# A fused attention and highway kernel: DMA transposes kept for nine slots, a gate bias added on the matrix engine in five, and two points without loads

## The chip, the cores and the metric

The kernel runs on one core of a Trainium2 chip. The core has five engines with one instruction stream each: TensorE (PE in the profile, with its weight loads as PEld), VectorE (DVE), ScalarE (ACT), GpSimd (POOL) and SyncE (SP). Each works in its own program order and waits for the others on semaphores. DMAs are issued by POOL (all loads, which cast float32 to float16 on the way) and by SP (stores and DMA transposes). The metric is the device time of one execution in microseconds; the time of a kernel is the median of its runs.

## What is computed

Inputs are q, k, v of shape (4, 6336, 256) and the weights of a highway layer. Cut to what matters:

```python
qn = q / (norm(q, axis=1) + 1e-6);  kn = k / (norm(k, axis=1) + 1e-6)
a = softmax(kn.T @ qn / tau)          # one 256 x 256 matrix per batch
x = (v @ a).reshape(25344, 256)
H = relu(x @ w_h);  T = sigmoid(x @ w_t + b_t)
out = T * H + (1 - T) * x
```

## The kernel before, in words

There are two kinds of work per batch b of 4. **Phase 1** (`p1_tile`, L197 to L203) goes over 49 row tiles of 128 rows and a rest of 64: six matmuls per tile sum S = k'q and the Gram diagonals G, from which the norms come. Then a **chain** (`chain`, ten steps) turns S and G into the matrix mr, which holds a, a w_h and a w_t side by side: squared norms on DVE (L221), a power and an addition on POOL (`norms`, L237 and L238), the reciprocal on DVE (L242), a diagonal matrix on ACT (L251), a matmul that spreads it (cq, L264), the logits on DVE (L269), two exponentials on ACT (L280), the row sums' reciprocal on DVE (L291), the scaled rows on ACT (L300), a transpose on PE (L310), its copy (L319), the product with the weights (ah, L326) and two copies (L337, L339). The exponential needs another ACT table than the sigmoid, so two table loads of ACT stand around it.

**Main slots.** Each slot t (0 to 99, 25 per batch, two row tiles each) takes the transposed rows of v and runs `mains` three times (L435): four matmuls each into z (one of two PSUM banks in turn), h and x (a ring of three banks, `hx_tile`). Then `elementwise_ops`: ACT takes the sigmoid of z (tt, L486) and copies the bias over the bank again, so that the next matmuls into it add to the bias (L490, from btb, for slot t + 2); DVE forms th from h and tt (L498) and ux from tt and x (L503); POOL subtracts them into the output tile (L510). So z of slot t + 2 stands behind the ACT work of slot t, x of slot t behind th of slot t - 1, and h of slot t behind ux of slot t - 2.

**Transposes of v.** For slots below TD = 66, PE transposes the rows three slots ahead (`transpose`, L412, four matmuls between z and h of slot t, for slot t + 3, into a single PSUM bank vtps), and ACT (even slots) or DVE (odd ones) copies the result to SBUF as vts (`vt_copy`, L427). For slots 66 to 99 SP issues DMA transposes in eight groups (`dma_transposes`, L375 and L386, tiles vtd and vtr), which use buffers of the rings of q and k.

**Order.** The program is written out by hand, one slot after another; each engine keeps that order. Phase 1 of batch b + 1 is spread over the slots of batch b, its last tile standing in slots 18, 43 and 63. A planner at build time holds loads in the list `want`, sorted by the slot in which they are due. `next_loads` issues up to two after each slot (four ahead of the first chain), where buffers and eight load lanes allow it, and a model of the arrival times (`landed`) decides how many tiles of phase 1 stand in a slot. Chain steps are hung into the slots by `STEPS`; for the last batch the norms stand ahead of slot 64, the reciprocal ahead of 66, cq after the matmuls of 66, the logits ahead of 68, the exponentials after the elementwise work of 68, the scaled rows after that of 69, the transpose after 71, its copy ahead of 72, ah after 73 and the copies ahead of 74. Batch 3 is slots 75 to 99. The v of a batch comes in three loads of 16, 16 and 17 row tiles; v1 is the second load of batch 0, used by slots 8 to 15 and so by the transpose that stands in slot 5. v11 is the last load of all, v10 the one before it.

Of the kernel before, what the change touches and what calls it, by code (L numbers as in the profile page):

```python
# [9 lines left out]
AluOp = mybir.AluOpType  # L10
# [5 lines left out]
P = 128  # L16
# [3 lines left out]
def kernel(  # L20
# [30 lines left out]
    def spans(*sizes):  # L51
# [24 lines left out]
    P1_END = [19, 44, 64]  # L76


    TD = 66
    TGROUPS = [  # L80
        (2, 32, 8, 57), (2, 40, 9, 61), (3, 0, 8, 65), (3, 8, 8, 69),
        (3, 16, 8, 73), (3, 24, 8, 77), (3, 32, 8, 81), (3, 40, 9, 85),
    ]
    LULL = [0, 0, 1, 7]


# [47 lines left out]

    load_q(0)
    load_k(0)
    bt_sb = const_pool.tile([1, C], f32, tag="bt")
    nc.sync.dma_start(out=bt_sb, in_=moe_b_t.rearrange("(a m) -> a m", a=1))


    ident0 = const_pool.tile([P, P], f32, tag="ident0")
# [70 lines left out]
    def chain(b):  # L212
# [102 lines left out]

        def at_copy():
            at_sb = work_pool.tile([P, 2, C], f16, tag="at_sb", bufs=1, name=f"at_sb{b}")
            cp = nc.vector.tensor_copy if b == 0 else nc.scalar.copy
            cp(out=at_sb, in_=st["at"])  # L319
            st["at_sb"] = at_sb  # L320

# [43 lines left out]
    def dma_transposes(t):  # L365

        for n, (b, s0, ns, at) in enumerate(TGROUPS):
            if at != t:
                continue
            g = max(i for i in range(len(VG[b])) if VG[b][i][0] <= s0)  # L370
            o = s0 - VG[b][g][0]
            assert o + ns <= VG[b][g][1]
            tag = "qk"[n % 2] + "_in"
            vt = stream_pool.tile([P, QTILES, C], f16, tag=tag, bufs=QRING, name=f"vtd{n}")
            nc.sync.dma_start_transpose(  # L375
                out=vt[:, 0:ns, :].rearrange("p s (c r) -> p (s c) r", c=2),
                in_=v_t[VFIRST[b] + g][:, o : o + ns, :].rearrange("p s c -> p (s c)"),
            )
            for j in range(ns):
                vT_dma[b, s0 + j] = vt[:, j, :].rearrange("p (c r) -> p c r", c=2)  # L380
            note(ns, 0.0)
            if s0 + ns == VG[b][g][0] + VG[b][g][1]:
                used.add(("v", VFIRST[b] + g))
            if s0 + ns == NS:
                vr = const_pool.tile([P, 2, REM], f16, tag=f"vtr{b}", name=f"vtr{b}")
                nc.sync.dma_start_transpose(out=vr, in_=rem_t["v"][0:REM, b, :])  # L386
                vT_dma[b, NS] = vr

    def vT_of(t, u):
        b, i = divmod(t, NPAIR)  # L390
        return vT_t[t][:, u] if t < TD else vT_dma[b, 2 * i + u]
    on_dve = {t + LOOK for e, o in zip(P1_END, STEPS[1:]) for t in (e + o[4], e + o[4] + 1)}
    o_t = {}
    NSLOT = B * NPAIR
# [35 lines left out]
    def mains(t, dst, off, seeded):  # L430
        b, i = divmod(t, NPAIR)
        mr = mr_t[b]
        for u, r in enumerate(nrows(i)):
            for kt in range(2):
                nc.tensor.matmul(  # L435
                    dst[0:r, u, :], vT_of(t, u)[:, kt, 0:r], mr[:, kt, off : off + C],
                    start=(not seeded and kt == 0 and (u == 0 or i == NPAIR - 1)),
                    stop=(kt == 1 and (u == 1 or i == NPAIR - 1)),
                    skip_group_check=seeded,
                )  # L440
# [42 lines left out]
    def elementwise_ops(t, z, h, x, ps):  # L483
# [2 lines left out]
        nc.scalar.activation(out=tt, in_=z, func=Act.Sigmoid)  # L486
        if ps is not None:
            vt_copy(t + LOOK, ps)
        if t + 2 < NSLOT:
            nc.scalar.copy(out=z, in_=btb)  # L490
        th = work_pool.tile([P, 2, C], f32, tag="th", bufs=5, name=f"th{t}")
        ux = work_pool.tile([P, 2, C], f32, tag="ux", bufs=5, name=f"ux{t}")
# [41 lines left out]
    for m in range(1, len(VALL)):  # L534
        b, g = VALL[m]
        at = b * NPAIR + VG[b][g][0] // 2 - LOOK - 1
        for bb, s0, _, slot in TGROUPS:
            if (bb, s0) == (b, VG[b][g][0]):
                at = slot - 1
        dep = ("v", m - VRING) if m >= VRING else None  # L540
        want.append((at, len(want), load_v, m, dep, VG[b][g][1]))
    want.sort()
# [6 lines left out]
    landing = [0.0] * LANES  # L549
    landed = {}  # L550
    dma_at = [0.0]

    def note(tiles, now):
        dma_at[0] = max(dma_at[0], now) + tiles * TILE_US
# [4 lines left out]
        landed[key] = dma_at[0]  # L559

    def next_loads(k, now):
        while k and want:
            _, _, fn, arg, dep, tiles = want[0]
            if dep is not None and dep not in ready:
                return
            if landing[-LANES] > now + SLACK:
                return
            want.pop(0)
            fn(arg)
            note_load((fn, arg), tiles, now)  # L570
            k -= 1
# [10 lines left out]
    zbank = []  # L582
    btb = const_pool.tile([P, 2, C], f32, tag="btb")

    def seed_banks():


        btp = hx_tile("btp")
        nc.tensor.matmul(btp[:, 0, :], ones32[0:1, :], bt_sb, start=True, stop=True)
        for u in range(2):  # L590
            nc.scalar.copy(out=btb[:, u, :], in_=btp[:, 0, :])
        for i in range(2):
# [8 lines left out]
    for j in range(NS + 1):  # L601
        p1_tile(0, j)
        if j == QG[0][1][0]:
# [3 lines left out]
            load_rem("q", q)  # L607
            load_rem("k", k)
            seed_banks()
            preload_table(Act.Sqrt)  # L610
        if j == QG[0][2][0]:
            load_q(QFIRST[1])
# [33 lines left out]
    for t in range(NSLOT):  # L646
        b, i = divmod(t, NPAIR)
        ready = set(used)
        run(t, "pre")
        z = zbank[t % 2]  # L650
        mains(t, z, 2 * C, True)
        dma_transposes(t)
        ps = transpose(t + LOOK) if t + LOOK < TD else None
        h = hx_tile(f"h{t}")
        mains(t, h, C, False)
        x = hx_tile(f"x{t}")
# [35 lines left out]
                for at, (when, fn) in zip(STEPS[pb + 1], chain(pb + 1)):  # L692
                    hooks.setdefault((t + 1 + at, when), []).append(fn)

        next_loads(2, now)
        room = DEFER - sum(t >= at for at in DRAIN)
        out_now = 0
        while len(stores) > room and out_now < 2:
# [40 lines left out]
```

## Time and profile before

| | |
|---|---|
| median of 13 runs | 290.46 us (288.11 to 308.25) |
| the profiled execution: time, span in the profile | 288.66 us, 286.9 us |
| PE busy | 256.8 us (90% of the span) |
| POOL, DVE, ACT busy | 168.7, 162.5, 159.4 us |
| granted TensorE clock over the span, mean | 0.973 |
| POOL's DMA queue (loads) | 39.19 MB, 68.7% of 16 engines' span |
| SP's DMA queue (stores, DMA transposes) | 30.35 MB, 33.5% |
| transposes of v: by PE, by DMA | 66 slots (264 matmuls), 34 slots (8 groups and 2 rests) |

The profile is one execution on the hardware profiler. Busy time is by engine; a group of instructions is named by its line, engine and tiles ("zbank<-mr,vts" is a matmul of mr and vts into the bank of z). Times in a timeline count from the span's start. Where a row has a bracket, the engine stood idle that long before it, and the name behind the arrow is what ended the idle time.

### The profile page before, as it was taken

The numbers are of one execution on the slowest core, as the hardware profiler recorded it, in microseconds if no ns is written. First come the engines' busy times: TensorE is split into PE (matmuls) and PEld (weight loads), VectorE is DVE, ScalarE is ACT, GpSimd is POOL, SyncE is SP. The second block draws the span as 40 slices with busy tenths as digits, with TensorE's granted clock in tenths as the row PEclk, the third lists the DMA queues.
The fourth block names the chain that finished last, engine by engine and source line by source line (L and its number), as shares of the span: only waits on it lengthen the run. The fifth ranks groups of instructions, "written<-read, shape, count | busy, mean of one in ns | idle before, by whom it ended". The sixth has DMA issues, their size and how long they took to land. (4 is left out here: it accounts for less than half of the span.)

```text
span 286.9 us, 6644 instructions
## 1 busy us (share of the span) xinstructions
PE 256.8 (90%) x2708; PEld 222.6 (78%) x2708; DVE 162.5 (57%) x307; ACT 159.4 (56%) x286; POOL 168.7 (59%) x181
## 2 busy tenths in 40 slices
PE   0699886999999999999999999999999569999990
PEld 0479763999999877899999877899998346788870
DVE  1000034974455684766666774555568347899992
ACT  1040036853453688465656687445457388799970
POOL 8122230797564774566569774445454745899991
PEclk9999997999999999999999999999999897999996
DMA  6999999999999999999999999999999999999996
GB/s 98 210 211 213 207 214 212 212 215 219 211 219 210 285 229 270 268 306 268 250 265 221 277 243 266 261 310 258 233 159 267 179 245 283 279 355 238 278 378 235
DMA packets 32577, 69.97 MB, mean 244 GB/s; under 512 B 19105, under 2 KB 21154, under 8 KB 28066
## 3 DMA queue, kind: packets, MB, share of 16 engines
q0 software_dynamic: 10288, 39.19, 68.7%
q1 hardware_dynamic: 22258, 30.35, 33.5%
q8 instruction: 21, 0.34, 0.4%
q14 instruction: 10, 0.08, 0.1%
HBM read 78.38 MB, written 25.95 MB: 364 GB/s over the span
## 5 line engine op out<-in xcount | busy, mean ns | idle before, releaser
L510 POOL TENSOR_TENSOR o<-th,ux 128x512 f32<-128x512 f32 x96 | 123.7, 1294 | 72.0 <-DVE ux L503 61.1
L197 PE MATMUL S<-q,k 128*128 128x256 f16 x392 | 88.3, 279 | 11.5 <-DMA k<-in_k_dram 11.5
L498 DVE SCALAR_TENSOR_TENSOR th<-h,tt 128x512 f32<-128x512 f32 (+1 forms) x104 | 69.0, 667 | 51.0 <-PE h L435 26.3
L486 ACT ACTIVATE tt<-zbank 128x512 f32<-128x512 f32 x100 | 59.6, 596 | 68.8 <-PE zbank L435 65.3
L435 PEld LDWEIGHTS <-vts 128*128 128x128 f16 (+1 forms) x792 | 72.0, 98 | 9.9 <-issue 3.1
L200 PE MATMUL G<-k 128*128 128x128 f16 x392 | 77.2, 223 | 0.2 <-DVE junk L221 0.2
L503 DVE SCALAR_TENSOR_TENSOR ux<-tt,x 128x512 f32<-128x512 f32 (+1 forms) x104 | 67.9, 656 | 0.1
L490 ACT COPY zbank<-btb 128x512 f32<-128x512 f32 x98 | 58.4, 595 | 2.2
L203 PE MATMUL G<-q 128*128 128x128 f16 x392 | 55.0, 223 | 0.0
L197 PEld LDWEIGHTS <-k 128*128 128x128 f16 x392 | 39.1, 100 | 16.4 <-DMA k<-in_k_dram 12.3
L435 PEld LDWEIGHTS <-vtd 128*128 128x128 f16 x396 | 39.6, 101 | 11.3 <-issue 5.2
L435 PE MATMUL zbank<-mr,vts 128*128 128x256 f16 x264 | 40.3, 274 | 0.6 <-DVE mr L339 0.6
L200 PEld LDWEIGHTS <-k 128*128 128x128 f16 x392 | 39.1, 100 | 1.1 <-issue 0.3
L435 PE MATMUL h<-mr,vts 128*128 128x256 f16 x264 | 39.9, 273 | 0.0
L435 PE MATMUL x<-mr,vts 128*128 128x256 f16 x264 | 39.9, 273 | 0.0
L427 DVE CAST vts<-vtps 128x512 f16<-128x512 f32 x33 | 22.7, 688 | 21.3 <-PE vtps L412 21.3
L203 PEld LDWEIGHTS <-q 128*128 128x128 f16 x392 | 30.9, 100 | 2.6
L412 PE MATMUL vtps<-ident,v 128*128 128x128 f16 x260 | 25.2, 221 | 0.0
L435 PE MATMUL x<-mr,vtd 128*128 128x256 f16 x132 | 21.1, 284 | 3.5 <-DVE th L498 3.5
L221 DVE SCALAR_TENSOR_TENSOR junk<-G,ident 128x128 f32<-128x128 f32 x16 | 3.7, 287 | 35.8 <-PE G L203 35.8
L112 POOL DMA_DIRECT2D q<-in_q_dram x25 | 14.2, 567 | 12.1 <-DMA q<-in_q_dram 5.7
L412 PEld LDWEIGHTS <-v 128*128 128x128 f16 x260 | 19.8, 98 | 1.8 <-issue 0.4
(73 smaller groups left out, 165.3 us busy)
## 6 DMA issues: line engine op xcount, KB each, us to landing
out_dram<-o SPq DMA_DIRECT2D x23, 1024.0 KB, 9.7
v<-in_v_dram POOLq DMA_DIRECT2D x8, 1024.0 KB, 26.7
q<-in_q_dram POOLq DMA_DIRECT2D x15, 512.0 KB, 25.7
k<-in_k_dram POOLq DMA_DIRECT2D x15, 512.0 KB, 25.9
v<-in_v_dram POOLq DMA_DIRECT2D x4, 1088.0 KB, 24.1
q<-in_q_dram POOLq DMA_DIRECT2D x7, 576.0 KB, 19.5
k<-in_k_dram POOLq DMA_DIRECT2D x7, 576.0 KB, 19.7
out_dram<-o SPq DMA_DIRECT2D x4, 256.0 KB, 5.3
```

What stands on the lines that cost most here:

```text
L112: nc.gpsimd.dma_start(out=q_t[n][:, 0:ns, :], in_=rows(q[b])[:, s0 : s0 + ns, :])
L197: nc.tensor.matmul(S[:, c, :], kc, qq[0:nr, :], start=first and c == 0, stop=last and c == 1)
L200: nc.tensor.matmul(G[:, c, :], kc, kc, start=first and c == 0, stop=False)
L203: nc.tensor.matmul(G[:, 2 + c, :], qc, qc, start=False, stop=last and c == 1)
L412: nc.tensor.matmul(ps[:, u, c, 0 : nr[u]], vt[0 : nr[u], bass.ts(c, P)], ident[0 : nr[u], 0 : nr[u]], start=(u == 0 and c == 0), stop=(u = ...
L427: cp(out=sb, in_=ps)
L435: nc.tensor.matmul(dst[0:r, u, :], vT_of(t, u)[:, kt, 0:r], mr[:, kt, off : off + C], start=(not seeded and kt == 0 and (u == 0 or i == NP ...
L486: nc.scalar.activation(out=tt, in_=z, func=Act.Sigmoid)
L490: nc.scalar.copy(out=z, in_=btb)
L498: nc.vector.scalar_tensor_tensor(out=th[pr, us, :], in0=h[pr, us, :], scalar=0.0, in1=tt[pr, us, :], op0=AluOp.max, op1=AluOp.mult,)
L503: nc.vector.scalar_tensor_tensor(out=ux[pr, us, :], in0=tt[pr, us, :], scalar=1.0, in1=x[pr, us, :], op0=AluOp.subtract, op1=AluOp.mult,)
L510: last = sub.tensor_tensor(out=ot[pr, o0 + us.start : o0 + us.stop, :], in0=th[pr, us, :], in1=ux[pr, us, :], op=AluOp.subtract,)
```

## The change

- DMA transposes are kept for slots 66 to 74 alone (`BY_DMA`; two groups, now placed in slots 52 and 57 instead of 57 and 61). Slots 75 to 99 are transposed by PE in slots 72 to 96, and copied by DVE and ACT as in the slots below 66. Six groups and one rest of DMA transposes go.
- In slots 68 to 72 (`PE_BIAS`) the bias is put into the bank of z by two matmuls of 65 rows ahead of the four of z, instead of by the copy on ACT two slots earlier (in slots 66 to 70). The operands are prepared once, by a memset and some fifteen small DVE instructions (`bias_rows`) and three DMAs of the bias instead of one.
- `next_loads` isn't called after a slot in which the last tile of a phase 1 stands, nor after the slot behind it.
- Loads of v are held back by `V_HELD`: v10 until slot 67, v11 until slot 74. The test compares with the current slot, which is -1 ahead of slot 0, and with 0 for a load that isn't in the table. Loads behind a held one may pass it.
- The copy of the transposed softmax matrix goes from ACT to DVE in the last chain (L319). The load of the third part of batch 2's v is due three slots ahead of its first DMA transpose, and the planner counts a DMA transpose as 3.5 tiles instead of one.

In the built program the loads around slot 0 stand so on POOL: before, v1, q8, k8, q9 ahead of slot 0, and k9 and q10 after it; changed, q8, k8, q9, k9 ahead of slot 0, and v1 and q10 after it. Phase 1 of batch 1 stands in slots 3 to 18, two or three tiles in each, instead of slots 6 to 18 with three or four; the later phases are spread as before.

```diff
--- before.py
+++ after.py
@@ -76,11 +76,12 @@
     P1_END = [19, 44, 64]
 
 
-    TD = 66
-    TGROUPS = [
-        (2, 32, 8, 57), (2, 40, 9, 61), (3, 0, 8, 65), (3, 8, 8, 69),
-        (3, 16, 8, 73), (3, 24, 8, 77), (3, 32, 8, 81), (3, 40, 9, 85),
-    ]
+    BY_DMA = range(66, 75)
+    TGROUPS = [(2, 32, 8, 52), (2, 40, 9, 57)]
+
+    PE_BIAS = range(68, 73)
+
+    V_HELD = {10: 67, 11: 74}
     LULL = [0, 0, 1, 7]
 
 
@@ -134,8 +135,10 @@
 
     load_q(0)
     load_k(0)
-    bt_sb = const_pool.tile([1, C], f32, tag="bt")
-    nc.sync.dma_start(out=bt_sb, in_=moe_b_t.rearrange("(a m) -> a m", a=1))
+    bt_sb = const_pool.tile([65, C], f32, tag="bt")
+    nc.vector.memset(bt_sb, 0.0)
+    for r in (0, 32, 64):
+        nc.sync.dma_start(out=bt_sb[r : r + 1, :], in_=moe_b_t.rearrange("(a m) -> a m", a=1))
 
 
     ident0 = const_pool.tile([P, P], f32, tag="ident0")
@@ -315,7 +318,7 @@
 
         def at_copy():
             at_sb = work_pool.tile([P, 2, C], f16, tag="at_sb", bufs=1, name=f"at_sb{b}")
-            cp = nc.vector.tensor_copy if b == 0 else nc.scalar.copy
+            cp = nc.scalar.copy if 0 < b < B - 1 else nc.vector.tensor_copy
             cp(out=at_sb, in_=st["at"])
             st["at_sb"] = at_sb
 
@@ -378,7 +381,7 @@
             )
             for j in range(ns):
                 vT_dma[b, s0 + j] = vt[:, j, :].rearrange("p (c r) -> p c r", c=2)
-            note(ns, 0.0)
+            note(3.5 * ns, 0.0)
             if s0 + ns == VG[b][g][0] + VG[b][g][1]:
                 used.add(("v", VFIRST[b] + g))
             if s0 + ns == NS:
@@ -388,7 +391,7 @@
 
     def vT_of(t, u):
         b, i = divmod(t, NPAIR)
-        return vT_t[t][:, u] if t < TD else vT_dma[b, 2 * i + u]
+        return vT_dma[b, 2 * i + u] if t in BY_DMA else vT_t[t][:, u]
     on_dve = {t + LOOK for e, o in zip(P1_END, STEPS[1:]) for t in (e + o[4], e + o[4] + 1)}
     o_t = {}
     NSLOT = B * NPAIR
@@ -430,6 +433,12 @@
     def mains(t, dst, off, seeded):
         b, i = divmod(t, NPAIR)
         mr = mr_t[b]
+        if t in PE_BIAS and seeded:
+            for u in range(2):
+                nc.tensor.matmul(
+                    dst[:, u, :], ones_hl, bt_hl, start=(u == 0), stop=False,
+                    skip_group_check=True,
+                )
         for u, r in enumerate(nrows(i)):
             for kt in range(2):
                 nc.tensor.matmul(
@@ -486,7 +495,7 @@
         nc.scalar.activation(out=tt, in_=z, func=Act.Sigmoid)
         if ps is not None:
             vt_copy(t + LOOK, ps)
-        if t + 2 < NSLOT:
+        if t + 2 < NSLOT and t + 2 not in PE_BIAS:
             nc.scalar.copy(out=z, in_=btb)
         th = work_pool.tile([P, 2, C], f32, tag="th", bufs=5, name=f"th{t}")
         ux = work_pool.tile([P, 2, C], f32, tag="ux", bufs=5, name=f"ux{t}")
@@ -534,9 +543,8 @@
     for m in range(1, len(VALL)):
         b, g = VALL[m]
         at = b * NPAIR + VG[b][g][0] // 2 - LOOK - 1
-        for bb, s0, _, slot in TGROUPS:
-            if (bb, s0) == (b, VG[b][g][0]):
-                at = slot - 1
+        if (b, VG[b][g][0]) == TGROUPS[0][:2]:
+            at = TGROUPS[0][3] - 3
         dep = ("v", m - VRING) if m >= VRING else None
         want.append((at, len(want), load_v, m, dep, VG[b][g][1]))
     want.sort()
@@ -549,6 +557,7 @@
     landing = [0.0] * LANES
     landed = {}
     dma_at = [0.0]
+    slot = [-1]
 
     def note(tiles, now):
         dma_at[0] = max(dma_at[0], now) + tiles * TILE_US
@@ -559,13 +568,14 @@
         landed[key] = dma_at[0]
 
     def next_loads(k, now):
-        while k and want:
-            _, _, fn, arg, dep, tiles = want[0]
-            if dep is not None and dep not in ready:
+        while k and want and landing[-LANES] <= now + SLACK:
+            for i, (_, _, fn, arg, dep, tiles) in enumerate(want[:5]):
+                held = fn is load_v and V_HELD.get(arg, 0) > slot[0]
+                if not held and (dep is None or dep in ready):
+                    break
+            else:
                 return
-            if landing[-LANES] > now + SLACK:
-                return
-            want.pop(0)
+            want.pop(i)
             fn(arg)
             note_load((fn, arg), tiles, now)
             k -= 1
@@ -582,11 +592,37 @@
     zbank = []
     btb = const_pool.tile([P, 2, C], f32, tag="btb")
 
+
+
+    ones_hl = const_pool.tile([65, P], f16, tag="ones_hl")
+    bt_hl = const_pool.tile([65, C], f16, tag="bt_hl")
+    bt_r = const_pool.tile([65, C], f32, tag="bt_r")
+
+    def bias_rows():
+        nc.vector.memset(ones_hl.bitcast(u16), 0)
+        nc.vector.memset(bt_hl.bitcast(u16), 0)
+        part = work_pool.tile([65, C], f16, tag="bt_part", bufs=1)
+        rest = bt_sb
+        for r, one, scale in ((0, 1.0, 2.0**11), (32, 2.0**-11, 8.0), (64, 2.0**-14, None)):
+            nc.vector.tensor_scalar(
+                out=ones_hl[r : r + 1, :], in0=ones32[r : r + 1, :], scalar1=one,
+                scalar2=None, op0=AluOp.mult, op1=AluOp.bypass,
+            )
+            nc.vector.tensor_copy(out=part, in_=rest)
+            nc.vector.tensor_copy(out=bt_hl[r : r + 1, :], in_=part[r : r + 1, :])
+            if scale is not None:
+                nc.vector.tensor_tensor(out=bt_r, in0=rest, in1=part, op=AluOp.subtract)
+                nc.vector.tensor_scalar(
+                    out=bt_r, in0=bt_r, scalar1=scale,
+                    scalar2=None, op0=AluOp.mult, op1=AluOp.bypass,
+                )
+                rest = bt_r
+
     def seed_banks():
 
 
         btp = hx_tile("btp")
-        nc.tensor.matmul(btp[:, 0, :], ones32[0:1, :], bt_sb, start=True, stop=True)
+        nc.tensor.matmul(btp[:, 0, :], ones32[0:1, :], bt_sb[0:1, :], start=True, stop=True)
         for u in range(2):
             nc.scalar.copy(out=btb[:, u, :], in_=btp[:, 0, :])
         for i in range(2):
@@ -607,6 +643,7 @@
             load_rem("q", q)
             load_rem("k", k)
             seed_banks()
+            bias_rows()
             preload_table(Act.Sqrt)
         if j == QG[0][2][0]:
             load_q(QFIRST[1])
@@ -646,11 +683,14 @@
     for t in range(NSLOT):
         b, i = divmod(t, NPAIR)
         ready = set(used)
+        slot[0] = t
         run(t, "pre")
         z = zbank[t % 2]
         mains(t, z, 2 * C, True)
         dma_transposes(t)
-        ps = transpose(t + LOOK) if t + LOOK < TD else None
+        ps = None
+        if t + LOOK < NSLOT and t + LOOK not in BY_DMA:
+            ps = transpose(t + LOOK)
         h = hx_tile(f"h{t}")
         mains(t, h, C, False)
         x = hx_tile(f"x{t}")
@@ -692,7 +732,9 @@
                 for at, (when, fn) in zip(STEPS[pb + 1], chain(pb + 1)):
                     hooks.setdefault((t + 1 + at, when), []).append(fn)
 
-        next_loads(2, now)
+
+        if t not in (end1 - 1, end1):
+            next_loads(2, now)
         room = DEFER - sum(t >= at for at in DRAIN)
         out_now = 0
         while len(stores) > room and out_now < 2:
```

## The prediction, as put on record before the result

> **What bounds the kernel now.** I read the table of stages first, then each engine's timeline where PE idles.
>
> The table of stages gives, per stretch of the span, the busy time of PE, PEld, DVE, ACT and POOL with their instructions, the granted clock and the DMA share. The first and the fourth row stand for two kinds of slot, the second and third for the last chain:
>
> ```profile
> 50.65:59.85 9.20, 9.20 (x98) 8.38 (x96) 9.03 (x16) 8.16 (x16) 7.87 (x10) 1.00 1.04 210
> ...
> 223.00:226.60 3.60, 0.25 (x3) 0.00 (x0) 0.25 (x2) 0.71 (x3) 2.76 (x4) 1.00 0.84 160
> 226.60:230.40 3.80, 3.77 (x17) 2.58 (x18) 2.11 (x4) 2.24 (x4) 2.83 (x3) 0.55 1.14 201
> ...
> 250.00:260.00 10.00, 10.00 (x94) 8.96 (x92) 9.80 (x16) 9.11 (x16) 9.88 (x9) 1.00 0.99 329
> ```
>
> PE is the bound nearly everywhere: from 49.1 to 222.7 its timeline shows only two rows with an idle time ahead of them (0.71 and 0.17 us), and from 240.9 to 279.9 none. What it loses lies at the start (loads of q and k), in the first chain, and in the last chain, 222.7 to 240.7. So an edit is worth what it adds to PE's work, or takes from those idle stretches.
>
> POOL's timeline (start, duration, instruction, idle time ahead) shows why PE stops at 223:
>
> ```profile
> 219.44 1.31 POOL L510 TENSOR_TENSOR o<-th,ux 128x512 f32<-128x512 f32 x1 [0.92 <-DVE ux L503]
> 223.74 0.57 POOL L124 DMA_DIRECT2D v<-in_v_dram  x1 [2.99 <-DMA vtd<-v]
> 224.33 1.03 POOL L237 TENSOR_TENSOR nrm<-n,half 128x4 f32<-128x4 f32 x1
> 225.44 0.20 POOL L238 TENSOR_TENSOR nrm<-nrm,eps 128x4 f32<-128x4 f32 x1
> ```
>
> The load v11 takes the buffer of a v that DMA transposes still read; it waits 2.99 us and issues for 0.57, with the power of the last chain behind it, though the squared norms were there at 220.2 (end of the last L221 row). PE's timeline shows what follows, with an earlier gap:
>
> ```profile
> 45.08 0.60 PE L310 MATMUL at<-ident,mr 128*128 128x128 f16 x4 [2.49 <-DVE mr L295]
> ...
> 226.63 1.04 PE L264 MATMUL cq<-dcat,taus 128*128 128x256 f32 x2 [3.38 <-ACT dcat L251]
> 227.47 1.06 PE L435 MATMUL zbank<-mr,vtd 128*128 128x256 f16 x4
> 228.32 1.06 PE L435 MATMUL h<-mr,vtd 128*128 128x256 f16 x4
> ...
> 230.59 0.60 PE L435 MATMUL h<-mr,vtd 128*128 128x256 f16 x4
> ...
> 237.15 1.01 PE L435 MATMUL x<-mr,vtd 128*128 128x256 f16 x4 [3.34 <-DVE th L498]
> ```
>
> Four matmuls that take 0.44 us from start to start elsewhere take 0.85 behind each gap: the clock is halved for some 3.4 us (granted 0.55 from 226.6 to 230.4, 0.57 from 45.5 to 49.5).
>
> **The change, part by part** (times of the span; minus is a gain).
>
> *1. No load ahead of the norms.* Last chain: POOL's output of slot 63 ends at 220.75, so the power starts there and not at 224.33, and is done with the addition at 222.1. DVE reaches the reciprocal behind ux of slot 65, at 223.0. From reciprocal to cq is 0.95 (225.68 to 226.63), so cq starts at 223.95: **-2.7**. PE then idles some 0.8 us, as in the middle chain that has the same form (0.71 at 102.72), and there the clock stayed full. From cq to the end of z of slot 68 took 3.96 (226.63 to 230.59); at the full clock it is 0.53 (cq at 102.72 to z at 103.25) + 1.31 for slot 67 + 0.44 = 2.28: **-1.7**. In the chain at 99 us the load ahead of the power took 0.57, and PE idled 0.71: **-0.6**. The third chain's power (164.35) had no load ahead; nothing.
>
> *2. Bias by PE.* Ten matmuls of 256 columns, as long as the others (0.11 each): 0.22 a slot. The pair of slot 68 stands ahead of the sigmoid that the exponentials wait for: **+0.2**. Those of 69 to 71 lie in the gap behind it. That of 72 costs +0.2 (counted in 3). For it ACT drops five copies; the one between the sigmoid of 68 and the table load (231.42 to 232.03) is on the path: **-0.6**. Then ACT's chain stands as it was: exponentials and table load, 3.7 us from 232.0 to 235.7, in which PE runs out of banks; the gap at 237.15 shrinks from 3.3 to about 2.5 and doesn't go. Sum up to x of slot 71 (240.03): -2.7 - 1.7 + 0.2 - 0.6 = **-4.8**.
>
> *3. Transposes back on PE.* The first row of the table above holds six slots of just this kind: transposes, no phase 1. PE's timeline has z of slots 1 and 5 at 50.65 and 56.79, and phase 1 behind slot 5 at 59.85: 9.20 / 6 = 1.53 us each. In the tail z follows z after 1.31 (254.23, 255.54). So 0.22 a slot. Slots 72 to 74: +0.66, with the bias of 72 +0.88, less 0.2 for x of 71 at full clock: z of slot 75 at **-4.1**. Slots 75 to 96: 22 x 0.22 = **+4.8**. Does an engine beside PE become the bound? DVE starts an instruction every 0.605 us when it is pressed (239.28, 239.89, 240.49, 241.09): five in two slots are 3.03, against PE's 3.07. In the six slots it lags its transposes by a constant 0.2. ACT idles 0.32 in every second slot there. I take PE, and keep +0.17 a slot as the other end: by DVE's durations (0.69 and 0.68) in place of its spacing, five make 3.4. The copy L319 on DVE (0.69) meets DVE's own idle time ahead of slot 74; nothing.
>
> *4. v1 late.* This is the term that the change's words do not name. The test for held loads holds every v ahead of slot 0, so v1 goes behind q8, k8, q9 and k9. POOL's queue is drained in order and its DMA engines are full (DMA share 1.04). Landings (issue plus time to landing): rem_v at 36.1 + 10.9 = 47.0, then v1 at 37.4 + 14.5 = 51.9, and q8 to k9, the last at 53.2 + 9.4 = 62.6. The same five transfers in the other order end at the same time, with v1 last: about **62.6**. Who waits: PE's transpose for slot 8, which stands in slot 5. PE gets there at 49.13 + 3 x 1.53 (slots 0 to 2) + 2 x 2.86 (slots 3 and 4, with three tiles of 0.44) + 0.44 (z) = 59.9. All of PE stands behind it: **+2.7**. (Bounds: 1.2 if v1 lands at 61.1, when the last packets of two transfers overlap; 3.5 if its semaphore comes 0.8 late.) Phase 1 standing earlier gives nothing back, since PE was never idle in these slots. Then the clock: the gap of 2.49 us at 45.08 was followed by half clock, which costs 1.7 in 3.4 us; one of 1.26 (at 32.79) was not. Between 0 and +1.7; the three half-clock stretches begin on a grid of about 3.4 us (45.9, 226.9, 237.1), and a gap that is cut by the grid may pass unseen, so I take the middle, **+0.9**.
>
> *5. The end.* DVE's last instruction ends at 281.4 and the span at 286.9. The last two stores land 4.0 and 3.5 us after issue; with the transposes gone the DMA engines have room, and the shortest landing of any store is 1.9. Between 0 and -1.6; I take **-1.0**.
>
> *Nothing:* the bias rows (some 17 small DVE instructions while DVE is busy 0.71 of the 30 us from 10 to 40). v10 now leaves POOL behind slot 67 (some 228.5) and must be there for the transposes in slot 77 (some 245); v11 took 12.7 from issue to landing, which leaves 4. v11 leaves at 245 for slot 88 at 262. If that cover failed, PE would wait in the tail. The two DMA transposes kept are issued earlier, and stores queue behind them on SP; output tile 62 needs one of these stores by 219, some 5 us after it should be through.
>
> **Sum:** -0.6 (middle chain) + 2.7 + 0.9 (v1) - 4.1 (last chain to slot 75) + 4.8 (tail) - 1.0 (end) = +2.7, so the profiled execution's 288.66 would be 291.4. The median stands 1.8 above that execution; I add the sum to it: 290.46 + 2.7 = **293.2 us**.
>
> **A rule weighed.** The Trainium skill's page "TensorE: Matmul & The Clock Gate", in Part 1: The HAM clock gate, has the array fall to half rate after at least one idle window of about 3.4 us of a free-running counter. A gap of 2.7 us would then never halve the clock, and the sum would be +1.8 (292.3). The row of 45.08, 2.49 us and then half clock, speaks against the strict form; by it alone the sum would be +3.5 (294.0).
>
> **Rivals.** *A, forecast: v1 late, tail bound by PE.* 291.5 to 295; chance 0.55. *B: v1 lands in time.* If the queue brings v1 by 59.9, the +3.6 of part 4 go and the sum is -0.9: 289.6, and 289.0 with the end at its bound. For it: transfers overlap at their ends, and a model of the same queue put phase 1 where it stands. Against it: 52 row tiles in 15.6 us (47.0 to 62.6) at a full DMA share. It decides from v1's landing alone: before 59.9 not slower, after about 61.5 slower. 0.27. *C: the tail isn't held by PE* but by DVE at 3.4 for two slots (+0.17 x 22 = +3.7 on A), or waits for v10: about 296.9; 0.18. That the change does not do what it says is excluded for the order (the power has no load ahead of it in the built program), not for the times.
>
> A measurement of this kernel tells a difference from none at about 0.5%, 1.45 us: faster is below 289.0, slower above 291.9. Of A some 0.04 lie below, 0.12 within, 0.39 above; of B 0.14, 0.13 and 0; of C 0, 0.02, 0.16. Together faster 0.18, same 0.27, slower 0.55. The range goes from B's better half, 288.3, to just short of C's middle, 296.3.
>
> **What would show it.** In the changed profile: PE idle 2 to 3.5 us near 60 ahead of a vtps matmul, released by a DMA of v (part 4; if that row is missing, B); the power right behind POOL's output of slot 63, cq idle under 1 us at full clock (part 1); PE still idle some 2.5 us behind the exponentials, released by th (part 2); z to z 1.53 in slots 76 to 95, with DVE not late by more than 0.3 (part 3; 1.6 or more is C); last DVE instruction to the span's end 4.5 us (part 5).

## The result, and the profile after

The changed kernel takes 296.36 us in the median of 11 runs (293.52 to 298.72); before takes 291.33 in the runs beside it. The ratio is **1.0186 (95%: 1.0151 to 1.0221)**, or +5.4 us: slower, as forecast, but by twice the +2.7, and just above the range's top. The profiled execution took 296.67 us with a span of 294.9. All ratios here and below leave out executions more than 1.5% above the fastest of their kernel, so a median over all runs can stand apart from them.

The starts of z in the two profiles (PE's timelines) give the places. Minus is earlier than before:

| | before | after | difference |
|---|---|---|---|
| first z (sigmoid of slot 0) | 49.76 | 48.91 | -0.85 |
| z of slot 19 | 98.77 | 101.56 | +2.79 |
| z of slot 64 | 219.15 | 226.00 | +6.85 |
| z of slot 75 | 246.36 | 249.31 | +2.95 |
| z of slot 99 | 277.85 | 285.83 | +7.98 |
| end of the span | 286.9 | 294.9 | +8.0 |

So, counted from the first z, the stretch with v1 cost 3.6 us, the first chain of a later batch and what follows it 4.1, the last chain gave back 3.9, and the tail cost 5.0. The 8.0 is over the ratio's 5.4 because before's profiled execution is 2.7 under its median.

PE's timeline of the changed kernel has these rows with over 0.6 us idle ahead (after the start-up):

```profile
45.03 0.60 PE L313 MATMUL at<-ident,mr 128*128 128x128 f16 x4 [2.50 <-DVE mr L298]
...
62.66 0.40 PE L415 MATMUL vtps<-ident,v 128*128 128x128 f16 x4 [3.47 <-DMA v<-in_v_dram]
...
108.22 0.86 PE L267 MATMUL cq<-dcat,taus 128*128 128x256 f32 x2 [3.42 <-ACT dcat L254]
...
230.79 0.70 PE L267 MATMUL cq<-dcat,taus 128*128 128x256 f32 x2 [0.69 <-ACT dcat L254]
239.24 0.60 PE L444 MATMUL x<-mr,vtd 128*128 128x256 f16 x4 [2.28 <-DVE th L507]
242.18 0.60 PE L444 MATMUL x<-mr,vtd 128*128 128x256 f16 x4 [1.24 <-DVE th L507]
```

The second row is v1, late as forecast. The fourth is the last chain: 0.69 us, where before idled 3.38. The third is new: the same wait for the diagonal matrix, but in the chain at 105 us, where before idled 0.71. The table of stages (columns as above) shows the clock behind these gaps:

```profile
59.19:62.66 3.47, 0.00 (x2) 0.01 (x1) 0.00 (x0) 0.60 (x1) 2.64 (x4) 1.00 0.98 203
62.66:69.49 6.83, 6.83 (x81) 6.33 (x82) 3.31 (x6) 3.17 (x6) 3.90 (x5) 1.00 1.04 214
104.80:108.22 3.42, 0.01 (x1) 0.00 (x0) 0.76 (x2) 0.74 (x3) 3.34 (x4) 1.00 1.08 222
108.63:112.05 3.42, 3.42 (x19) 2.16 (x18) 3.03 (x6) 2.64 (x5) 2.00 (x3) 0.50 0.99 212
...
230.79:234.59 3.80, 3.80 (x32) 3.31 (x33) 3.22 (x6) 2.10 (x4) 2.44 (x3) 1.00 0.67 276
255.00:265.00 10.00, 10.00 (x106) 9.10 (x105) 10.00 (x18) 8.91 (x17) 8.50 (x8) 1.00 0.97 252
```

Behind the wait for v1 the clock stays full (1.00). Behind the new gap it is half (0.50), and PE issues 19 matmuls in 3.42 us. Behind cq of the last chain it is full, where before had 0.55. In the last row, the tail, PE is busy all the time, and so is DVE.

POOL's timeline tells why the norms are late at 105 us, and on time in the last chain:

```profile
102.84 0.57 POOL L125 DMA_DIRECT2D v<-in_v_dram  x1 [2.60 <-DMA k<-in_k_dram]
103.43 2.52 POOL L519 TENSOR_TENSOR o<-th,ux 128x512 f32<-128x512 f32 x2
105.91 1.04 POOL L240 TENSOR_TENSOR nrm<-n,half 128x4 f32<-128x4 f32 x1
...
226.29 1.31 POOL L519 TENSOR_TENSOR o<-th,ux 128x512 f32<-128x512 f32 x1 [0.94 <-DVE ux L512]
227.54 1.03 POOL L240 TENSOR_TENSOR nrm<-n,half 128x4 f32<-128x4 f32 x1
```

The first row is v5, the load of 17 tiles. Before issues it behind the norms (POOL's timeline, then PE's row of cq):

```profile
100.39 1.06 POOL L237 TENSOR_TENSOR nrm<-n,half 128x4 f32<-128x4 f32 x1
...
102.90 0.62 POOL L124 DMA_DIRECT2D v<-in_v_dram  x1
```

```profile
102.72 0.70 PE L264 MATMUL cq<-dcat,taus 128*128 128x256 f32 x2 [0.71 <-ACT dcat L251]
```

In the changed kernel it stands some slots earlier, waits 2.60 us for an earlier load to land, and two output tiles and the power of the chain queue behind it. In the last chain the power follows the output tile directly.

### The profile page after: what moved, and what is told of

Its sections match the earlier page's. It is cut to its first block, busy times and chain, and to the rows that moved or that the text cites. A ratio compares the mean times of both kernels' runs of the same rounds, so it can differ in the third digit from the quotient of the medians.

```text
span 294.9 us, 6895 instructions
## 1 busy us (share of the span) xinstructions
PE 261.5 (89%) x2818; PEld 228.4 (77%) x2818; DVE 173.7 (59%) x338; ACT 160.3 (54%) x292; POOL 169.1 (57%) x181
## 5 line engine op out<-in xcount | busy, mean ns | idle before, releaser
L444 PEld LDWEIGHTS <-vts 128*128 128x128 f16 (+1 forms) x1092 | 100.2, 98 | 14.1 <-issue 4.1
L499 ACT COPY zbank<-btb 128x512 f32<-128x512 f32 x93 | 55.7, 599 | 1.6
L444 PE MATMUL zbank<-mr,vts 128*128 128x256 f16 (+1 forms) x364 | 55.6, 275 | 0.5 <-DVE mr L342 0.4
L444 PE MATMUL x<-mr,vts 128*128 128x256 f16 (+1 forms) x364 | 55.4, 274 | 0.0
L444 PE MATMUL h<-mr,vts 128*128 128x256 f16 (+1 forms) x364 | 55.4, 274 | 0.0
L430 DVE CAST vts<-vtps 128x512 f16<-128x512 f32 x45 | 30.9, 688 | 21.9 <-PE vtps L415 21.8
L415 PE MATMUL vtps<-ident,v 128*128 128x128 f16 x358 | 34.7, 220 | 3.5 <-DMA v<-in_v_dram 3.5
L415 PEld LDWEIGHTS <-v 128*128 128x128 f16 x358 | 27.2, 98 | 6.5 <-DMA v<-in_v_dram 3.7
L430 ACT CAST vts<-vtps 128x512 f16<-128x512 f32 x43 | 24.9, 580 | 3.3 <-PE vtps L415 3.3
L119 POOL DMA_DIRECT2D k<-in_k_dram x25 | 13.6, 545 | 10.1 <-DMA k<-in_k_dram 5.7
## 6 DMA issues: line engine op xcount, KB each, us to landing
q<-in_q_dram POOLq DMA_DIRECT2D x7, 576.0 KB, 20.5
```

Of the source, the lines that this page charges most:

```text
L415: nc.tensor.matmul(ps[:, u, c, 0 : nr[u]], vt[0 : nr[u], bass.ts(c, P)], ident[0 : nr[u], 0 : nr[u]], start=(u == 0 and c == 0), stop=(u = ...
L430: cp(out=sb, in_=ps)
L444: nc.tensor.matmul(dst[0:r, u, :], vT_of(t, u)[:, kt, 0:r], mr[:, kt, off : off + C], start=(not seeded and kt == 0 and (u == 0 or i == NP ...
```

## The experiments

My theory after the result: both the wait at 62.7 us and the late norms at 105.9 come from the hold test, which keeps v1 off POOL's queue ahead of slot 0. All loads behind it then go out one place earlier in the list, and reach the load lanes too early. The rival: two losses with nothing in common, or a tail that sets the end whatever comes ahead.

**e1_v1_early: v1 back ahead of slot 0, all else as changed.**

```diff
-                held = fn is load_v and V_HELD.get(arg, 0) > slot[0]
+                held = fn is load_v and V_HELD.get(arg, -1) > slot[0]
```

> The changed kernel with one thing put right: a load is held only if its tensor has a held load for a later slot, so the second v load goes out ahead of slot 0 again and everything else of the change stays. My theory has two losses that both come from that hold: PE's wait of 3.47 us for the second v tile at 62.7 us, and the late norms of the first chain of the second batch (PE idle 3.42 us before cq at 108.2 us and the half-clock stretch after it, some 4 to 5 us together), because with one load less ahead of slot 0 the sixth v load is issued before the norms on GpSimd's queue. Then both go: ratio to before about 0.99 to 1.00 (288 to 291 us on before's 291.3), 7 us under the changed kernel at most. Rival 1, only the first wait comes from the hold and the norms are late for another reason: 3.5 us under the changed kernel, ratio about 1.007. Rival 2, the tail sets the end whatever the loads do: no change, ratio 1.015 to 1.02.

Measured: 289.82 us, ratio to before 0.9976 (0.9940 to 1.0011), 2.1% or 6.1 us under the changed kernel. Both gaps are gone. POOL's timeline, then PE's row of cq:

```profile
98.59 1.28 POOL L519 TENSOR_TENSOR o<-th,ux 128x512 f32<-128x512 f32 x1 [1.14 <-DVE ux L512]
99.93 1.04 POOL L240 TENSOR_TENSOR nrm<-n,half 128x4 f32<-128x4 f32 x1
```

```profile
102.37 0.70 PE L267 MATMUL cq<-dcat,taus 128*128 128x256 f32 x2 [0.32 <-ACT dcat L254]
```

The power has no load ahead of it and PE idles 0.32 us. So both losses come from the hold test, as the theory had it; the rest of the change, with v1 in time, is about neutral.

**e6_v5_later: v1 late as changed, but v5 kept behind the norms.**

```diff
-        if t not in (end1 - 1, end1):
+        if t not in (end1 - 1, end1, 16, 17):
             next_loads(2, now)
```

> The changed kernel with the second v load late as it is, but with no loads issued in slots 16 and 17 either, so that the sixth v load stands behind the norms of the first chain on GpSimd's queue. It parts the two losses that e1_v1_early took away together. My theory: the wait of 3.47 us for the second v tile stays; the 3.4 us idle before cq of that chain and the half-clock stretch go, 4 to 5 us under the changed kernel: ratio to before 1.002 to 1.005. Rival, the norms are late because the whole kernel is 3 us behind its loads by then, and the load's place does nothing: ratio 1.015 to 1.02, cq still waiting 3 us for the ScalarE copy.

Measured: ratio 1.0076 (1.0030 to 1.0123), halfway between e1_v1_early and the changed kernel, and 3.2 us under the latter where 4 to 5 had been expected. POOL's timeline:

```profile
102.65 1.31 POOL L519 TENSOR_TENSOR o<-th,ux 128x512 f32<-128x512 f32 x1 [1.21 <-DVE ux L512]
103.91 1.05 POOL L240 TENSOR_TENSOR nrm<-n,half 128x4 f32<-128x4 f32 x1
...
109.29 0.62 POOL L125 DMA_DIRECT2D v<-in_v_dram  x1
```

The norms follow the output tile, and cq has no idle time over 0.6 us ahead of it. That parts the 6.1 us: 1.0186 - 1.0076 = 1.1%, **3.2 us, for v5 ahead of the norms**; 1.0076 - 0.9976 = 1.0%, **2.9 us, for the stretch with the late v1**. Each of these differences carries some +-0.6%. PE's wait for v1 is only 1.71 us in this profile (at 63.54), but the stretch isn't shorter: from the first z to that of slot 19 it takes 53.1 us, 53.3 in the changed kernel and 49.7 in before (by the sigmoids), since half clock between slots 0 and 1 had cost 1.5 us ahead of the wait.

**e3_tail_by_pe: before, with the transposes from slot 75 on by PE.**

```diff
-    TD = 66
-    TGROUPS = [
-        (2, 32, 8, 57), (2, 40, 9, 61), (3, 0, 8, 65), (3, 8, 8, 69),
-        (3, 16, 8, 73), (3, 24, 8, 77), (3, 32, 8, 81), (3, 40, 9, 85),
-    ]
+    BY_DMA = range(66, 75)
+    TGROUPS = [(2, 32, 8, 57), (2, 40, 9, 61)]
...
```

> The kernel before with one part of the change alone: the v transposes of the slots from 75 on go back from DMA to PE. My prediction priced them at 0.22 us for each of 22 slots, so 4.8 us: ratio about 1.0165 (296.1 us on 291.3), the slot pace in the tail 1.53 us in place of 1.31 us, and PE the engine that is waited for. Rival, the tail is held by VectorE and not by PE, so the PE transposes are half hidden: ratio 1.00 to 1.01. Second rival, without the DMA transposes the last output's landing is earlier by 1 us (my fifth step) and the ratio is 1.013.

Measured: ratio 1.0172 (1.0103 to 1.0240), +5.0 us for the +4.8 of the prediction. The second rival, an earlier end, lies inside this interval (1.013), but not in the profile: from the sigmoid of slot 99 to the end of the span it is 8.2 us here (285.26 to 293.5) as in before (278.65 to 286.9).

**e2_skip_only: before, with no loads around a chain's root.**

```diff
-        next_loads(2, now)
+        if t not in (end1 - 1, end1):
+            next_loads(2, now)
```

> The kernel before with one part of the change alone: no loads are issued in the two slots around a chain's root. All DMA transposes and the bias copy stay as before. My prediction priced this at 4.4 us in the last chain (the root 2.7 us earlier and no half-clock stretch of 1.7 us after it) and 0.6 us in the middle one: ratio about 0.983 (286.3 us on 291.3). Rival, the loads that are put off are late instead and PE waits for a q, k or v tile after the chain: ratio 0.99 to 1.00, with a PE idle row ended by DMA within the slots that follow the chains.

Measured: ratio 0.9995 (0.9950 to 1.0040): nothing, where I had expected -5.0 us. Ahead of the last chain's matmuls all is as it should be (cq at 224.21 with 0.69 us idle, where before has 226.63), but PE's timeline shows the gain handed back:

```profile
261.06 0.61 PE L435 MATMUL zbank<-mr,vtd 128*128 128x256 f16 x4 [0.64 <-DMA vtd<-v]
274.29 0.61 PE L435 MATMUL zbank<-mr,vtd 128*128 128x256 f16 x4 [2.57 <-DMA vtd<-v]
```

In this profile some 2 us go before the tail: the sigmoid of slot 70 comes 4.1 us ahead of before's and that of slot 75 1.8, behind two gaps ahead of x (3.04 and 1.25 us) and half clock from 234.2 to 241.1. In the tail PE then gets to its transposed tiles too soon. The records of the DMA queues give an estimate: one group for four slots is 2048 packets of 256 bytes, and such groups moved at 512 packets a us (4096 from 256 to 264 us), so 4.0 us; the stores of four slots are 1 MB, and moved at 1.62 MB in 4 us (252 to 256 us of before), so 2.6 us. Together 6.6 us of all DMA engines, against 4 x 1.31 = 5.24 us of PE. It is on the high side, since 0.6 MB of stores moved beside those 4096 packets. By it the DMAs are the slower side of the tail in before too, and only their lead hides it.

**e4_skip_bias_dma: before, with the skip and the bias by PE; all DMA transposes kept.** The edit is that of e2_skip_only with `PE_BIAS`, `bias_rows` and the DVE copy of L319 as in the change.

> The kernel before with the skip of loads around a chain's root and the bias of five slots by PE (with its weight copy on VectorE), while all DMA transposes of before stay and no v load is held. By my steps: 4.4 us and 0.6 us gained by the skip, some 0.4 us by the bias in the chain, nothing lost in the tail and no late v tile: ratio about 0.981 (285.8 us on 291.3), under both kernels. Rival, the bias by PE costs more matmul time than the ScalarE copies were worth: the same ratio as the skip alone or up to 0.5 us above it.

Measured: ratio 1.0006 (0.9964 to 1.0048), missed like e2_skip_only. The execution that was profiled took 309.98 us, and its trace shows why that one is so long, in PE's timeline and POOL's; where the gain of the skip goes in the others it doesn't show.

```profile
239.27 1.03 PE L444 MATMUL zbank<-mr,vtd 128*128 128x256 f16 x4 [14.67 <-DMA vtd<-v]
```

```profile
244.05 0.61 POOL L125 DMA_DIRECT2D v<-in_v_dram  x1 [16.87 <-DMA vtd<-v]
```

PE waits 14.67 us for a transposed tile and v11 16.87 us for its buffer, while the DMA engines move 102 GB/s in the mean (208 to 250 us). e9_v1_late_only, below, has the same in its trace.

**e8_skip_last_by_pe: e2_skip_only, its last nine slots by PE.**

```diff
+    BY_DMA = range(66, 91)
     TGROUPS = [
         (2, 32, 8, 57), (2, 40, 9, 61), (3, 0, 8, 65), (3, 8, 8, 69),
-        (3, 16, 8, 73), (3, 24, 8, 77), (3, 32, 8, 81), (3, 40, 9, 85),
+        (3, 16, 8, 73), (3, 24, 8, 77),
     ]
...
```

> The kernel of e2_skip_only (before with no loads around a chain's root) with the last nine slots' transposes by PE, all others from slot 66 on by DMA. In e2_skip_only the chain gained some 4 us up to slot 72 and PE then waited for DMA-transposed tiles, 0.64 us at 261 us and 2.57 us at 274 us, because SyncE's queue issues them one after the other behind the stores and was busy without a break from 225 us on. If that queue takes the skip's gain back, then leaving out its two last groups lets most of it through: -4.4 + 9 x 0.22 = -2.4 us, ratio about 0.992 (289.2 us). Rival, the gain is lost before that by the chain itself (x waits 3 us and the clock is halved): ratio 1.002 to 1.007, since the PE transposes are paid and nothing comes back.

Measured: ratio 0.9971 (0.9922 to 1.0019), between the two. It was wrong to look for the lateness in the two last groups alone. PE's timeline has it one group earlier, 3.82 us:

```profile
261.52 0.61 PE L435 MATMUL zbank<-mr,vtd 128*128 128x256 f16 x4 [3.82 <-DMA vtd<-v]
```

The chain kept its gain here (sigmoid of slot 75 at 242.46, 4.5 us ahead of before's), so the rival is out. It looks as if the rate of groups in a row counts, and not the last ones. That leads to groups with gaps:

**e5_half_tail_dma: e1_v1_early, twelve more slots by DMA, in three groups of four with four PE slots between.**

```diff
-    BY_DMA = range(66, 75)
-    TGROUPS = [(2, 32, 8, 52), (2, 40, 9, 57)]
+    BY_DMA = [*range(66, 79), *range(83, 87), *range(91, 95)]
+    TGROUPS = [
+        (2, 32, 8, 52), (2, 40, 9, 57), (3, 0, 8, 65), (3, 16, 8, 73), (3, 32, 8, 81),
+    ]
```

> The kernel with the second v load ahead of slot 0 (e1_v1_early) and, besides the chain's nine slots, twelve of the tail's slots, in three groups of four with gaps between them, transposed by DMA. My theory: each slot by DMA takes 0.22 us off PE, so 12 x 0.22 = 2.6 us under e1_v1_early, as long as SyncE's queue keeps up; it took some 9.3 us for a group of four slots with the stores between them, and eight slots, half of them by PE, last 8 x 1.42 = 11.4 us. So about 0.989 of before (288.3 us on 291.5), under both kernels. Rival, the DMA transposes come late in the tail as they did in e2_skip_only, and PE waits for a transposed tile 2 to 3 us: ratio 0.997 or above.

Measured: 287.63 us, ratio **0.9862 (0.9812 to 0.9911)**, the best of all and under both kernels; 3.3 us under e1_v1_early by the ratios, for 2.6 expected. The tail in its table of stages:

```profile
242.00:277.00 35.00, 35.00 (x344) 31.25 (x344) 33.96 (x58) 29.99 (x53) 30.80 (x26) 1.00 0.93 307
```

PE is never idle in it, and the DMA share has room (0.93).

**e10_more_tail_dma: e5_half_tail_dma, and the last five slots by DMA too,** so nine in a row.

```diff
-    BY_DMA = [*range(66, 79), *range(83, 87), *range(91, 95)]
+    BY_DMA = [*range(66, 79), *range(83, 87), *range(91, 100)]
...
+        (3, 40, 9, 86),
```

> The kernel of e5_half_tail_dma with the last five slots by DMA too, so that nine slots in a row (91 to 99) are. In the traces a group of four slots takes some 4 us of all DMA engines (2048 packets of 256 bytes at 512 a us) and the four slots' stores 1 MB at 0.4 MB a us another 2.6 us, together 6.6 us against 5.24 us of PE for four slots by DMA; so nine in a row fall behind PE by some 3 us, and what the five slots save on PE, 5 x 0.22 = 1.1 us, is lost to a wait: ratio 0.986 to 0.996, PE idle before a zbank matmul for a DMA-transposed tile. Rival, the lead that the PE slots in between have built up covers it: ratio 0.982, with no such wait.

Measured: ratio 0.9900 (0.9863 to 0.9937), with the wait where it was expected:

```profile
272.35 0.61 PE L447 MATMUL zbank<-mr,vtd 128*128 128x256 f16 x4 [2.78 <-DMA vtd<-v]
```

The rival's 0.982 is excluded: nine in a row fall behind, as the estimate has it. More transposes off PE saved nothing more.

**e7_no_pe_bias: e1_v1_early with the bias by the ScalarE copy again.**

```diff
-    PE_BIAS = range(68, 73)
+    PE_BIAS = ()
```

> The kernel with the second v load ahead of slot 0 (e1_v1_early), without the bias by PE: the five slots get their bias by the ScalarE copy again. My prediction gave the bias by PE +0.2 us of matmuls and -0.6 us by the copies off ScalarE in the chain, so this should be 0.4 us slower than e1_v1_early: ratio 0.999 on 0.9976. Rival, without the matmuls PE idles longer ahead of x in the chain's slots, over 2.5 us within one window, and half a window of full clock is lost: 1.5 to 2 us slower. Second rival, the PE bias does nothing or costs: the same or up to 0.5 us faster.

Measured: ratio 0.9964 (0.9926 to 1.0003), against 0.9976 with it. It can't be told from nothing. The gap ahead of x is 3.04 us there, 2.28 and 1.14 with the bias by PE: the idle time is split, and not less.

**e9_v1_late_only: before, with no v load ahead of slot 0.**

```diff
...
+            for i, (_, _, fn, arg, dep, tiles) in enumerate(want[:5]):
+                held = fn is load_v and slot[0] < 0
+                if not held and (dep is None or dep in ready):
+                    break
...
```

> The kernel before with one thing of the change alone: no v load is issued ahead of slot 0 (what the change's hold test does by its default), and nothing else. The changed kernel against e1_v1_early, and e6_v5_later between them, price this at some 3 us by PE's wait for the second v tile and some 3 us by the late norms of the first chain, together 6.1 us: ratio to before about 1.02 (297 us on 291.3), with PE idle 3 us or more ahead of the second v tile's transposes and again ahead of cq of the first chain. Rival, the late load costs only its own wait as my prediction had it, 2.7 to 3.6 us: ratio 1.009 to 1.012, and the norms are late only together with the skip's other order.

Measured: 318.30 us (313.13 to 320.81 in all six runs), ratio 1.0772 (1.0709 to 1.0835), which goes by the two shortest. Both theories missed by 16 us or more. POOL's timeline, and the DMA view of 208 to 250 us (its GB/s row has 40 slices; the column of the issues is the median time to landing):

```profile
251.14 0.57 POOL L124 DMA_DIRECT2D v<-in_v_dram  x1 [25.87 <-DMA vtd<-v]
251.73 1.03 POOL L237 TENSOR_TENSOR nrm<-n,half 128x4 f32<-128x4 f32 x1
```

```profile
GB/s 122 23 34 29 28 34 65 41 30 44 62 47 22 130 29 53 24 53 71 20 26 30 178 32 16 32 18 290 125 40 86 310 158 88 84 94 62 77 85 289
DMA packets 4378, 3.24 MB, mean 77 GB/s; under 512 B 4111, under 2 KB 4111, under 8 KB 4111
...
vtd<-v SPq DMA_TRANSPOSE x2, 43.2
```

While the load of v10 and the transposes are under way together, little moves: 77 GB/s where other stages have over 200, and 43 us to the landing of a transpose. v11 waits 25.87 us for the buffer that they read, with the norms behind it: the wait of 2.99 us that the prediction showed in before, grown more than eightfold.

The first chain of a later batch shows something too, in POOL's timeline and PE's row of cq:

```profile
101.38 0.57 POOL L124 DMA_DIRECT2D v<-in_v_dram  x1 [1.67 <-DMA k<-in_k_dram]
```

```profile
107.25 0.70 PE L264 MATMUL cq<-dcat,taus 128*128 128x256 f32 x2 [0.54 <-ACT dcat L251]
```

v5 goes out ahead of the norms here as well (the power starts at 104.94), and yet they are hardly late: DVE has the squared norms ready at 104.5, 3.1 us after v5 got its lane. In the changed kernel they are ready at 102.6, and v5 gets its lane at 102.84. So v5's place alone isn't the loss, and on this the rival was right: it takes a lane that comes free later than the squared norms, as in the changed kernel. What makes the lane that much later there is open.

**e11_late_v_held: e9_v1_late_only with the change's holds.**

```diff
-                held = fn is load_v and slot[0] < 0
+                held = fn is load_v and V_HELD.get(arg, 0) > slot[0]
```

> The kernel of e9_v1_late_only with the change's holds added: the last two v loads wait for slots 67 and 74; all DMA transposes stay. In e9_v1_late_only the DMA engines moved only 77 GB/s from 208 to 250 us, while the tenth v load and the first transposes were under way together, a transposed packet of 256 bytes took 0.12 us in the mean and up to 5 us, PE waited 14 us for transposed tiles and the last v load 25.9 us for its buffer. If it is the load beside the transposes that does this, holding the load takes it away: 25 us faster than e9_v1_late_only, ratio to before 1.00 to 1.025. Rival, the transposes are slow by themselves or beside the stores: ratio stays at 1.06 to 1.08 with the same waits.

Measured: ratio 1.0227 (1.0166 to 1.0287), 16 us under e9_v1_late_only for 25 expected. The same DMA view, 208 to 250 us:

```profile
DMA packets 10842, 8.01 MB, mean 191 GB/s; under 512 B 10003, under 2 KB 10195, under 8 KB 10195
...
vtd<-v SPq DMA_TRANSPOSE x5, 10.9
```

With the load of v10 held, five groups go through where two did, in a quarter of the time each. So the jam is the load beside the transposes. What tips it over is open: the profiled executions of before, e9_v1_late_only and e4_skip_bias_dma all issue v10 5.1 us behind the first transposes (194.98 and 200.10; 199.51 and 204.62; 197.64 and 202.76), and that of before didn't jam. With the hold v11 goes out at 248.07, beside the transposes of the tail: those issued at 251.75 take 14.16 us to go out, and PE waits 6.74 us for a transposed tile at 268.66. That this is the same jam in small is a guess.

**e12_no_hold: e1_v1_early without holds.**

```diff
-    V_HELD = {10: 67, 11: 74}
+    V_HELD = {}
```

> The kernel of e1_v1_early without holds: the tenth and eleventh v loads go out as soon as they may, all else as in the change. Theory: two groups of transposes are left, issued five slots earlier; the tenth v load meets the second of them, so packets get slower and z of slots 66 to 70 waits for a transposed tile: 2 to 14 us slower than e1_v1_early, ratio 1.005 to 1.045. Rival, by then the transposes are far enough ahead and the hold is worth nothing: ratio 0.997 as e1_v1_early. My prediction had put no price on the hold at all.

Measured: ratio 0.9950 (0.9909 to 0.9992), as the rival said. But the ratio goes by six of the twelve executions. The other six took 297.8 to 305.3 us (median of all 295.02), about as the theory said; e1_v1_early, with the hold, has none above 291.9 in twelve. Before has such executions too, 13 of 48 with 299.2 to 309.5 us, and the changed kernel has none above 298.72. No trace here shows one of before or of this kernel. e4_skip_bias_dma, which has no hold either, was profiled in one (309.98 us), and there it is the jam; that it is so in the others is likely, but not shown.

## Why the forecast was too low

The failed step is in part 1, "**In the chain at 99 us ... -0.6**". It took the place of every other load ahead of that chain as in before. Part 4 had just moved one of them. The gain was there once v1 was put right (0.32 us idle in e1_v1_early for before's 0.71), but in the changed kernel it is a loss of 3.2 us (e6_v5_later).

| step | forecast | measured |
|---|---|---|
| v1 late, with the clock (part 4) | +3.6 | +2.9 by the ratios; in the profile +3.6 from the first z, +2.8 from the start of the span |
| chain at 99 us (part 1) | -0.6 | **+3.2** by the ratios, +4.1 in the profile |
| last chain to slot 75 (parts 1 to 3) | -4.1 | -3.9 in the profile |
| tail (part 3) | +4.8 | +5.0 (e3_tail_by_pe, and the profile) |
| end (part 5) | -1.0 | 0 |

- **v1 (part 4).** The mechanism and the place were right, and the load landed as forecast (62.66 for 62.6). PE waited 3.47 us and not 2.7 because it got there at 59.19 and not at 59.9: the first z came 0.85 us earlier, since the gap of 2.50 us at 45.03 was followed by full clock in this execution (granted 1.00 from 45.5 to 49.5, for before's 0.57). That is luck, and the wait took it back. The +0.9 for the clock was 0 here; behind the waits for v1 in e9_v1_late_only (2.28 us) and e11_late_v_held (2.80 us) the clock was halved for one window, so both ends of that range occur.
- **The skip (part 1).** Right in the last chain. But the price was not free to add to any tail: alone, beside all DMA transposes, it gives nothing (e2_skip_only). What it gains there is lost to waits for transposed tiles and to the clock. With the DMA engines relieved it stays, and the same change relieves them by moving transposes back to PE. The prediction charged the move +4.8 us and saw only a cost in it.
- **Bias by PE (part 2).** A net gain of 0.4 us in the forecast, not resolved here (e7_no_pe_bias).
- **The tail (part 3).** 1.53 us a slot as forecast. Rival C's bound didn't come, though DVE is as full as PE there.
- **The end (part 5).** DVE's last instruction ends 5.5 us ahead of the span's end in both profiles. The last transposes of before land at 274 us, some 7 us before DVE ends, so they weren't beside the last stores.
- **The hold.** I had put it down as a risk of late tiles alone. Beside a late v1 it is worth 16 us (e9_v1_late_only and e11_late_v_held). With v1 in time the ratio of e12_no_hold shows nothing, but half of its executions are 5.9 us or more above the longest of e1_v1_early.
- **Rival B**, v1 in time, was priced at 0.9 us under before. e1_v1_early is this case: 0.7 us under (0.24%; by the interval 1.7 under to 0.3 over).

## What to carry to other kernels

When a load is moved, price what stands behind every later load of that queue as well: a queue with a fixed number of lanes makes an early load wait, and compute on the issuing engine waits with it. Before a gain on the busiest engine is added up, sum what a hidden stage (here 6.6 us of DMA for 5.24 us of PE) needs for the same work: it takes back what exceeds its lead, and a mix of both ways in turns (e5_half_tail_dma) beat either. Keep loads away from DMA transposes.

## What was not expected of the hardware

**The clock.** The half-clock stretches of one execution begin whole multiples of 3.41 us apart and last one or two such windows (behind long waits more, 20.5 us in e9_v1_late_only). Whether a gap halves the clock depends on where the grid cuts it. In e5_half_tail_dma 2.28 us of idle PE lie within one window; in e8_skip_last_by_pe 3.04 us are cut into 1.50 and 1.54:

```profile
230.01:232.29 2.28, 0.00 (x1) 0.00 (x0) 0.74 (x2) 1.44 (x2) 0.20 (x1) 1.00 0.81 162
232.59:236.00 3.41, 3.37 (x17) 2.23 (x16) 1.84 (x5) 2.54 (x5) 1.43 (x2) 0.50 1.01 243
```

```profile
229.79:232.83 3.04, 0.00 (x1) 0.00 (x1) 0.75 (x2) 2.76 (x5) 0.44 (x1) 1.00 1.05 194
232.83:239.66 6.83, 5.42 (x48) 4.45 (x48) 5.02 (x10) 5.93 (x12) 2.31 (x2) 1.00 1.08 295
```

The shorter gap is followed by clock 0.50, the longer one by 1.00. The 3.47 us ahead of v1, cut into 1.66 and 1.81, passed too. Over all these profiles the largest piece that passed was 1.81 us and the smallest that was followed by half clock 1.67 (with short idle times beside it): about half a window. The gap of 2.5 us ahead of the first chain's transpose, near 45 us, lies in one window in before and is followed by half clock; in the changed kernel the grid cuts it into 1.25 and 1.25, and it passes. One window at half clock costs 1.7 us, so one kernel may differ by that or a multiple from run to run; this is an estimate, from the profiles alone. The Trainium skill's page "TensorE: Matmul & The Clock Gate", Part 1: The HAM clock gate, asks for at least one idle window of about 3.4 us. The windows are as it says; the wholly idle one is not needed here (2.28 of 3.41 us).

**The jam.** Loads of 8 KB packets and DMA transposes of 256-byte packets, under way together, held each other at 77 GB/s for 42 us in e9_v1_late_only and at 102 in e4_skip_bias_dma, with the DMA engines shown as busy most of the while.
